# Another order for the first loads of a fused linear-attention and gated-MLP kernel

## The chip, the cores and the metric

The kernel runs on one core of a Trainium2 chip. Five engines work side by side on it, each with its own stream of instructions: PE (matmul), ACT (the scalar engine), DVE (the vector engine), POOL (GpSimd) and SP, which here only issues DMAs. Engines wait for each other through semaphores. The metric is the device time of one execution in microseconds; less is better. Before the change it was 221.64 us (median of three runs, 221.39 to 222.84).

## What is computed

The reference normalises x (2048 tokens of 512 values) and adds two branches to it. Cut to what matters:

```
xn = layernorm(x)                                   # 2048 x 512
q, k, v = split(xn @ wqkv)                          # 32 heads of 16
phi(a)  = [softmax(a @ w_phi), softmax(-a @ w_phi)] # per head, 16 + 16 features
kv, z   = sum_s phi(k)_s v_s^T,  sum_s phi(k)_s
attn    = (phi(q) kv) / (phi(q) z + 1e-6) @ wo
mlp     = ((xn @ w_gate) * (xn @ w_up)) @ w_down    # hidden width 1792
out     = x + attn + mlp
```

## The kernel before

Tokens are cut into 16 tiles of 128 (t = 0 to 15) and, for the MLP, into 4 groups of 512 (g); the hidden width into 14 column tiles of 128 (ft). A contraction over 512 is four matmuls (q = 0 to 3) that add up in one PSUM bank. These kinds of work return in the prediction:

- **Normalisation.** For t = 0 to 3 DVE takes the moments of the raw tile (L415, L416; the mean of t = 1 comes from ACT, L423), subtracts the mean (L430), PE transposes the centred tile by a product with the identity (four matmuls of 128 columns) and ACT copies it out (L277). For t = 4 and up DVE takes moments for four tiles at once (L452, L454), POOL makes the reciprocal root (L458, L460), DVE normalises (L481) and a DMA transpose puts the result into the transposed array.
- **k_pe(t)**: the value projection, four matmuls against `wv`, copied by ACT.
- **wprime(w)**: folds `w_phi` into the key (w = 1) or query (w = 0) weights: 16 matmuls of 128 columns, with a block-diagonal form of `w_phi` that POOL builds first (L395). After it **k_pk(t)** and **q_pk(t)** give the features in four matmuls; ACT makes both signs, DVE a tree of maxima (L519) and a subtraction (L525), ACT the exponential, DVE the sums (L539), a reciprocal (L568) and the product (L571). For keys the last three are k_norm(t).
- **glu(g, ft)**: a gate product and an up product, four matmuls of 512 columns each; ACT copies the gate out of its bank, DVE multiplies it with the up bank (L595) and so frees that bank. The units share three PSUM banks at first (5, 6, 7), later four, so a product waits for the ACT copy or the DVE multiply of an earlier unit.
- **emit_kv(half)**: sums over the key tiles of one half, 8 groups of 8 small matmuls. **q_num(t)** and **final(t)** finish the attention and the output.

All matmuls are issued by one helper, L297, all ACT copies by L277 and all DMAs by L165 (L164 for transposes).

The order of the work is not the order of the source. Each operation is recorded as a step; a planner (`_order`) then gives each engine a fixed order, by list scheduling on assumed costs. For a DMA the recorded argument `at` is the earliest time at which the planner takes the data to have landed. It changes nothing in the DMA itself, only where the planner puts the steps that use the data. Each engine works off its list strictly in order, and waits at the head of it.

All loads are issued by SP. The first ones of the kernel before are: x tiles 0, 1, and 2 with 3 in one transfer; the value weights in two halves of 256 rows; gate and up columns of the first four column tiles; x tiles 4 to 7; the feature weights `w_phi`; then the transposing load of the key weights, and the other gate and up columns. x tiles 8 to 15 are issued only when the DMA transpose of tile 7 has landed (`load_later`), with an assumed landing of 29.8 us.

k_pe(0) to k_pe(3) are recorded matmul by matmul, so that the planner may begin them with the rows that a first half of the value weights holds.

Of the kernel before, what the change touches and what calls it, by code (L numbers as in the profile page):

```python
# [12 lines left out]
PE, ACT, DVE, POOL, SP = "PE", "ACT", "DVE", "POOL", "SP"  # L13
# [168 lines left out]
def bass_parallel_sum__linear_kernel_hedgehog__glu_gated_bilinear__prompt_kernel(  # L182
    nc: bass.Bass,
    A_x: bass.AP,
    A_wqkv: bass.AP,
    A_w_phi: bass.AP,
    A_wo: bass.AP,
    B_x: bass.AP,
    B_w_gate: bass.AP,
    B_w_up: bass.AP,  # L190
    B_w_down: bass.AP,
    out: bass.AP,
):
    with ExitStack() as es:
        _build(nc, es, A_x, A_wqkv, A_w_phi, A_wo, B_w_gate, B_w_up, B_w_down, out)


def _build(nc, es, A_x, A_wqkv, A_w_phi, A_wo, B_w_gate, B_w_up, B_w_down, out):
# [59 lines left out]
    def sbv(name, lo, n):  # L258
        off = layout[name] + lo
        return arena[:, off:off + n]  # L260
# [67 lines left out]
    wv_v = sbv("wv", 0, NQ * 512).rearrange("p (q j) -> p q j", q=NQ)  # L328
    wo_v = sbv("wo", 0, NQ * 512).rearrange("p (q j) -> p q j", q=NQ)
    wg_v = sbv("wg", 0, NQ * FF).rearrange("p (q f) -> p q f", q=NQ)  # L330
    wu_v = sbv("wu", 0, NQ * FF).rearrange("p (q f) -> p q f", q=NQ)
# [4 lines left out]
    def load_x(on, t0, n, at):  # L336
        return sc.dma(on, sbv("x", t0 * 512, n * 512).rearrange("p (t d) -> p t d", t=n),
                      x_flat[t0 * 128:(t0 + n) * 128, :].rearrange("(t p) d -> p t d", p=128), at=at)

    def load_w(on, dst, src, at, issue=500.0):  # L340
        return sc.dma(on, dst, src, at=at, issue=issue)

    def load_wT(w, at):

        return sc.dma(SP, wT_v[:, w, :, :], A_wqkv[:, w * 512:(w + 1) * 512], transpose=True, at=at, issue=4600.0)

    def load_gu(on, f0, n, at):
        return [load_w(on, v[:, :, f0 * 128:(f0 + n) * 128],
                       src[:, f0 * 128:(f0 + n) * 128].rearrange("(q p) f -> p q f", p=128), at)
                for v, src in ((wg_v, B_w_gate), (wu_v, B_w_up))]  # L350

    load_x(SP, 0, 1, 2950.0)
    load_x(SP, 1, 1, 3400.0)
    load_x(SP, 2, 2, 4700.0)
    wv_loads = [load_w(on, wv_v[:, 2 * h:2 * h + 2, :],
                       A_wqkv[h * 256:(h + 1) * 256, 1024:1536].rearrange("(q p) j -> p q j", p=128), at)
                for on, h, at in ((SP, 0, 5700.0), (SP, 1, 6600.0))]
    load_gu(SP, 0, 4, 9300.0)
    load_x(SP, 4, 4, 11400.0)
    sc.dma(SP, wphi_v, bass.AP(tensor=A_w_phi.tensor, offset=A_w_phi.offset, ap=[[16, 128], [2048, NQ], [1, 16]]),  # L360
           at=11600.0)
    load_wT(1, 13600.0)
    load_gu(SP, 4, 5, 17900.0)
    load_gu(SP, 9, 5, 22300.0)


# [568 lines left out]
```

## Time and profile before

| | before |
|---|---|
| time, median of three runs | 221.64 us (221.39 to 222.84) |
| profiled execution: span, first to last instruction | 219.2 us |
| granted TensorE clock, mean | 1.000 |
| HBM read, written | 8.67 MB, 2.10 MB |
| POOL busy | 10.7 us |

The span is what the page gives of the profiled execution's own time; the median of the runs is 2.4 us more, for what lies before the first and after the last instruction. Times in the profile count from the start of the span. Matmuls overlap, so a busy PE row does not tell how tightly they follow each other; that is read from the starts. In lists of instructions the bracket gives how long the engine sat idle before the instruction and what ended that.

### The profile page before, as it was taken

Reading aid. Unit: us, or ns where it says so; the run is one execution under the profiler, and the core shown is the slowest. Engines: PE = TensorE matmul, PEld = TensorE weight load, DVE = VectorE, ACT = ScalarE, POOL = GpSimd, SP = SyncE. Lnnn points to the kernel's source line nnn. Section 1 sums busy time; section 2 is a strip of 40 time slices with the busy share of each in tenths; the row PEclk is TensorE's granted clock in tenths of the full one; section 3 lists DMA queues with packets and bytes.
Section 4 is the critical chain, followed back from the end, with each engine's and each line's share of the span. In section 5 each row is a group of like instructions: output and inputs, shape, how many; then the busy total and the mean of one; then the engine's idle time right before and its main releaser. Section 6 shows DMA issues by size and latency. Waiting matters only on the chain.

```text
span 219.2 us, 3572 instructions
## 1 busy us (share of the span) xinstructions
PE 215.1 (98%) x1281; PEld 105.0 (48%) x1281; DVE 193.0 (88%) x549; ACT 115.5 (53%) x191; POOL 10.7 (5%) x29
## 2 busy tenths in 40 slices
PE   7999999999999999999999999999999999999995
PEld 6444444444445545444445444445444445444543
DVE  4477999999999389999999899999999999998432
ACT  4757987548453599965452885735453333230000
POOL 4431000010002000000000000000000000000000
DMA  5999550025901340000000003155367555656451
GB/s 169 325 227 354 95 178 1 3 56 145 326 0 23 78 96 3 0 0 0 3 0 1 3 0 65 30 99 106 80 129 99 121 119 119 100 122 141 96 76 48
DMA packets 47458, 19.91 MB, mean 91 GB/s; under 512 B 37456, under 2 KB 47440, under 8 KB 47440
## 3 DMA queue, kind: packets, MB, share of 16 engines
q1 hardware_dynamic: 47440, 19.69, 39.6%
q8 instruction: 10, 0.16, 0.3%
q14 instruction: 8, 0.07, 0.1%
HBM read 8.67 MB, written 2.10 MB: 49 GB/s over the span
## 4 chain that ended last, share of the span: by engine, by line
PE 96%; DMA 2%; SPq 1%; issue 0%; DVE 0%
PE ps L297 96%; DMA arena<-in_A_wqkv_dram 2%; SPq L165 1%; DVE arena L700 0%
## 5 line engine op out<-in xcount | busy, mean ns | idle before, releaser
L297 PE MATMUL ps<-arena 128*128 128x512 bf16 (+4 forms) x1281 | 215.1, 331 | 1.8 <-DVE arena L368 1.0
L297 PEld LDWEIGHTS ps<-arena 128*128 128x128 bf16 x1281 | 105.0, 99 | 111.8 <-ACT arena L277 1.3
L277 ACT ACTIVATE arena<-ps 128x512 bf16<-128x512 f32 (+1 forms) x136 | 71.8, 590 | 48.3 <-PE ps L297 40.0
L277 ACT ACTIVATE arena<-arena 128x1024 bf16<-128x1024 bf16 (+1 forms) x40 | 38.5, 977 | 28.4 <-DVE arena L525 28.3
L539 DVE TENSOR_TENSOR arena<-arena 128x512 f32<-128x512 bf16 (+3 forms) x128 | 49.0, 394 | 0.2
L595 DVE TENSOR_TENSOR arena<-ps,arena 128x512 bf16<-128x512 f32 x56 | 38.1, 680 | 2.7 <-PE ps L297 1.6
L519 DVE TENSOR_TENSOR arena<-arena 128x64 bf16<-128x64 bf16 (+3 forms) x128 | 31.4, 273 | 4.0 <-ACT arena L277 3.7
L525 DVE TENSOR_TENSOR arena<-arena 128x1024 bf16<-128x1024 bf16 x32 | 21.5, 676 | 0.1
L700 DVE TENSOR_TENSOR arena<-ps,arena 128x512 bf16<-128x512 f32 (+2 forms) x13 | 8.4, 648 | 7.1 <-PE ps L297 6.9
L452 DVE BATCH_NORM_STATS2 arena<-arena 128x6 f32<-128x512 bf16 x12 | 8.2, 688 | 3.5 <-DMA arena<-in_A_x_dram 3.5
L571 DVE TENSOR_TENSOR arena<-arena 128x1024 bf16<-128x1024 bf16 x16 | 10.9, 680 | 0.0
L277 ACT ACTIVATE arena<-ps,arena 128x512 bf16<-128x512 f32 x12 | 7.8, 682 | 2.8 <-PE ps L297 2.8
L568 DVE RECIPROCAL arena<-arena 128x64 bf16<-128x64 f32 x16 | 8.7, 546 | 0.0
L672 DVE TENSOR_TENSOR arena<-ps,arena 128x512 bf16<-128x512 f32 x12 | 8.1, 675 | 0.1
L664 DVE RECIPROCAL arena<-ps 128x32 f32<-128x32 f32 x16 | 5.6, 348 | 2.4 <-PE ps L297 2.4
L651 DVE TENSOR_TENSOR arena<-arena 128x512 bf16<-128x512 bf16 x16 | 6.6, 415 | 0.0
L648 DVE RECIPROCAL arena<-arena 128x32 f32<-128x32 f32 x16 | 5.4, 335 | 0.0
L481 DVE TENSOR_SCALAR arena<-arena 128x512 bf16<-128x512 bf16 x12 | 4.3, 401 | 0.5 <-POOL arena L460 0.5
L415 DVE BATCH_NORM_STATS2 arena<-arena 128x6 f32<-128x512 bf16 x4 | 2.8, 690 | 2.0 <-DMA arena<-in_A_x_dram 2.0
L458 POOL TENSOR_SCALAR arena<-arena 128x4 f32<-128x4 f32 x3 | 0.8, 259 | 50.7 <-DVE arena L454 50.7
L460 POOL TENSOR_TENSOR arena<-arena 128x4 f32<-128x4 f32 x3 | 3.2, 1051 | 0.3
L697 DVE SCALAR_TENSOR_TENSOR arena<-ps,arena 128x512 bf16<-128x512 f32 x4 | 3.0, 748 | 0.0
(29 smaller groups left out, 24.4 us busy)
## 6 DMA issues: line engine op xcount, KB each, us to landing
out_dram<-arena SPq DMA_DIRECT2D x15, 128.0 KB, 1.8
arena<-in_B_w_down_dram SPq DMA_DIRECT2D x1, 1792.0 KB, 7.5
arena<-in_B_w_gate_dram SPq DMA_DIRECT2D x2, 640.0 KB, 6.8
arena<-in_B_w_up_dram SPq DMA_DIRECT2D x2, 640.0 KB, 8.0
arena<-in_A_x_dram SPq DMA_DIRECT2D x1, 1024.0 KB, 6.2
arena<-arena SPq DMA_TRANSPOSE x44, 2.9
arena<-in_A_wqkv_dram SPq DMA_DIRECT2D x2, 256.0 KB, 3.6
arena<-in_B_w_gate_dram SPq DMA_DIRECT2D x1, 512.0 KB, 5.5
```

Source lines behind the costliest of these rows:

```text
L277: return e.activation(out=out_ap, in_=in_ap, func=func, scale=scale, **kw)
L297: ins = e.matmul(o, lhsT=l, rhs=r, start=a, stop=z)
L452: dve(lambda e, t=t: e.bn_stats(stats_v[:, t, 0:6], x_tile(t)), [x_tile(t)], [stats_v[:, t, 0:6]], 512)
L519: dve(lambda e, dst=dst, src=src, k=k: e.tensor_tensor(out=dst, in0=src[:, :, 0:k], in1=src[:, :, k:2 * k], op=ALU.max), [src], [dst], 16 ...
L525: dve(lambda e: e.tensor_tensor(out=p4, in0=p4, in1=src[:, :, None, :].to_broadcast([128, 16, 16, 4]), op=ALU.subtract), [pst, src], [pst] ...
L539: dve(lambda e, dst=dst, src=src, k=k: e.tensor_tensor(out=dst, in0=src[:, :, 0:k], in1=src[:, :, k:2 * k], op=ALU.add), [src[:, :, 0:2 * ...
L568: dve(lambda e: e.reciprocal(out=rs, in_=sm), [sm], [rs], 64, rate=6.0)
L571: dve(lambda e: e.tensor_tensor(out=e4, in0=e4, in1=r4[:, :, None, :].to_broadcast([128, 16, 16, 4]), op=ALU.mult), [ek_v[:, t, :], rs], [ ...
L595: dve(lambda e: e.tensor_tensor(out=dst, in0=bank(bu), in1=gr, op=ALU.mult), [bank(bu), gr], [dst], 512, prio=-1.0)
L651: dve(lambda e: e.tensor_tensor(out=e1, in0=e1, in1=rs[:, :, None, :].to_broadcast([128, 8, 16, 4]), op=ALU.mult), [e1, rs], [e1], 512, ra ...
L672: dve(lambda e: e.tensor_tensor(out=o4, in0=n4, in1=w4, op=ALU.mult), [nd[:, :, 0:64], w], [o], 512)
L700: dve(lambda e: e.tensor_tensor(out=og, in0=ob, in1=xs, op=ALU.add), [ob, xs], [og], c1 - c0, prio=-2.0)
```

## The change

Only the first loads differ. x tiles 2 and 3 come in two transfers instead of one; the value weights come whole instead of in two halves, and stand between them; the feature weights go ahead of x tiles 4 to 7. The number of DMAs (14 up to the last gate and up columns) and the bytes are the same. The assumed landings change too: the gate columns from 9.3 to 9.0 us, the up columns from 9.3 to 10.6 us, the feature weights from 11.6 to 10.9, x 4 to 7 from 11.4 to 12.2, the key weights from 13.6 to 14.0 us. Since the planner works with these, the order on PE, ACT and DVE changes in many places behind the start. The number of instructions on each of them stays the same.

```diff
-    def load_gu(on, f0, n, at):
+    def load_gu(on, f0, n, at, at_up=None):
         return [load_w(on, v[:, :, f0 * 128:(f0 + n) * 128],
-                       src[:, f0 * 128:(f0 + n) * 128].rearrange("(q p) f -> p q f", p=128), at)
-                for v, src in ((wg_v, B_w_gate), (wu_v, B_w_up))]
+                       src[:, f0 * 128:(f0 + n) * 128].rearrange("(q p) f -> p q f", p=128), a)
+                for v, src, a in ((wg_v, B_w_gate, at), (wu_v, B_w_up, at if at_up is None else at_up))]
 
     load_x(SP, 0, 1, 2950.0)
     load_x(SP, 1, 1, 3400.0)
-    load_x(SP, 2, 2, 4700.0)
-    wv_loads = [load_w(on, wv_v[:, 2 * h:2 * h + 2, :],
-                       A_wqkv[h * 256:(h + 1) * 256, 1024:1536].rearrange("(q p) j -> p q j", p=128), at)
-                for on, h, at in ((SP, 0, 5700.0), (SP, 1, 6600.0))]
-    load_gu(SP, 0, 4, 9300.0)
-    load_x(SP, 4, 4, 11400.0)
+    load_x(SP, 2, 1, 3850.0)
+    load_w(SP, wv_v, A_wqkv[:, 1024:1536].rearrange("(q p) j -> p q j", p=128), 5500.0)
+    load_x(SP, 3, 1, 5950.0)
+    load_gu(SP, 0, 4, 9000.0, 10600.0)
     sc.dma(SP, wphi_v, bass.AP(tensor=A_w_phi.tensor, offset=A_w_phi.offset, ap=[[16, 128], [2048, NQ], [1, 16]]),
-           at=11600.0)
-    load_wT(1, 13600.0)
+           at=10900.0)
+    load_x(SP, 4, 4, 12200.0)
+    load_wT(1, 14000.0)
     load_gu(SP, 4, 5, 17900.0)
     load_gu(SP, 9, 5, 22300.0)
```

## The prediction

> **What bounds the kernel now.** I read the page's busy table first, then the chain that ended last in order of time, then the start as a timeline, then the engines by stages.
>
> ```profile
> PE 215.1 (98%) x1281; PEld 105.0 (48%) x1281; DVE 193.0 (88%) x549; ACT 115.5 (53%) x191; POOL 10.7 (5%) x29
> ```
>
> The chain, as start, length and what:
>
> ```profile
> 2.69 4.04 DMA arena<-in_A_wqkv_dram
> 6.72 0.05 issue
> 6.77 210.16 PE ps L297 x1235
> ```
>
> The end is set by the second half of the value weights, which lands at 6.73 (2.69 + 4.04), and from then on by PE alone. Between 20.7 and 44.8 us PE starts 113 matmuls of 512 columns, 24.1 / 112 = 0.216 us apart; a product of four takes 0.863. Read by starts, PE waits after 4 us only at four places: 0.47 before the first and 0.35 before the second half of the value weights, 0.14 at 13.4, 0.10 at 14.4. So about 1.1 us is the most that the change can win; every new wait on PE is a loss.
>
> The start (start, length, instruction, idle before and what ended it):
>
> ```profile
> 4.35 0.90 PE L297 MATMUL ps<-arena 128*128 128x128 bf16 x12 [0.31 <-DVE arena L430]
> 5.56 1.03 PE L297 MATMUL ps<-arena 128*128 128x512 bf16 x7 [0.31 <-DMA arena<-in_A_wqkv_dram]
> 5.71 0.69 DVE L415 BATCH_NORM_STATS2 arena<-arena 128x6 f32<-128x512 bf16 x1
> 6.65 0.35 DVE L430 TENSOR_SCALAR arena<-arena 128x512 bf16<-128x512 bf16 x1
> 6.77 7.45 PE L297 MATMUL ps<-arena 128*128 128x512 bf16 x36 [0.18 <-DMA arena<-in_A_wqkv_dram]
> ```
>
> Loads, with KB and us from issue to landing:
>
> ```profile
> arena<-in_A_x_dram SPq DMA_DIRECT2D x1, 1024.0 KB, 6.2
> arena<-in_A_wqkv_dram SPq DMA_DIRECT2D x2, 256.0 KB, 3.6
> arena<-in_B_w_gate_dram SPq DMA_DIRECT2D x1, 512.0 KB, 5.5
> arena<-in_B_w_up_dram SPq DMA_DIRECT2D x1, 512.0 KB, 6.9
> arena<-in_A_x_dram SPq DMA_DIRECT2D x1, 512.0 KB, 7.8
> arena<-in_A_x_dram SPq DMA_DIRECT2D x1, 256.0 KB, 2.8
> ```
>
> With the issues at 1.71 (x 2, 3), 2.18 and 2.65 (value weights), 3.20 (gate), 3.71 (up), 4.26 (x 4 to 7), 4.81 (feature weights) they land at 4.5, 5.4, 6.7, 8.7, 10.6, 12.06 and 12.3: in their order, as one stream.
>
> DVE, which is nearly as full as PE, where the order changes; and PE, PEld, DVE, ACT, POOL busy by stages:
>
> ```profile
> 20.31 1.24 DVE L519 TENSOR_TENSOR arena<-arena 128x512 bf16<-128x512 bf16 x4 [0.76 <-ACT arena L277]
> 32.78 0.69 DVE L452 BATCH_NORM_STATS2 arena<-arena 128x6 f32<-128x512 bf16 x1
> 35.81 0.68 DVE L595 TENSOR_TENSOR arena<-ps,arena 128x512 bf16<-128x512 f32 x1
> ```
> ```profile
> 45.00:71.00 26.00, 26.00 (x136) 12.03 (x134) 25.91 (x68) 13.80 (x22) 1.27 (x2) 1.00 0.39 114
> 71.00:77.00 6.00, 6.00 (x76) 3.53 (x73) 2.08 (x5) 3.29 (x12) 0.00 (x0) 1.00 0.40 80
> ```
>
> From 21 to 71 us DVE has no room to make up a delay; from 71 to 77 it has 3.9 us.
>
> **The loads, to 10 us.** x 2 takes half of what x 2, 3 took behind x 1 (x 1 is there at 3.39, 4.5 - 3.4 = 1.1, half 0.55): 3.95. DVE reaches it at 4.50 as before; nothing is won. The whole value weights take the two halves' 2.25 (6.73 - 4.5) and land at 6.2; with the gate-to-up step instead (10.6 - 8.7 = 1.9 for the same 512 KB) 5.85. x 3 closes the same 1024 KB as before: 6.7; bounds 6.2 and 7.0.
>
> PE's order here: two matmuls of k_pe(0), the transpose of x 2 (4 x 0.056 = 0.22), five matmuls, the transpose of x 3, nine matmuls. Before, the first three matmuls ran on the first half ahead of 6.77, so 13 and one transpose were left: 6.77 + 13 x 0.216 + 0.22 = 9.80. After: 6.2 + 7 x 0.216 + 0.22 = 7.93, then the transpose waits for x 3: moments to centred tile took 5.71 to 7.00, so 6.75 + 1.29 + 0.06 = 8.1. Then 0.22 and 9 x 0.216: 10.27. **+0.47**; with the early bounds 9.8 (0.0), with x 3 at 7.0 10.55 (+0.75). I take the middle, since the stream was steady.
>
> **Two small waits go.** Both gate products now come before the up product, needed at 12.0 and not 10.67; the up columns land at 10.6, so no wait either way. The third gate product no longer follows at once on a bank that DVE must free (-0.14), and wprime, which waited for POOL's block-diagonal form (12.40 + 1.84 = 14.24), comes at 15.4, with w_phi landing earlier (-0.10). x 4 to 7 land 0.3 later (what w_phi takes, 12.3 - 12.06); DVE has idled 3.5 us there. Issues on SP: the same ten, each hidden behind the stream. PE after the start: 0.47 - 0.24 = **+0.22**.
>
> **The order from 17 us.** The gate product of (0, 4) moves ahead of k_pk(0 to 3), the up product of (0, 5) behind k_pk(4 to 7). So k_pk(0) comes 0.86 + 0.22 = 1.08 later and DVE's tree starts at 21.4 instead of 20.31: idle that DVE cannot use. k_pe(4) comes 0.64 earlier, 24.12; its transposed tile landed at 24.1, behind the weights in the stream (0 to 0.2; I take 0).
>
> On DVE the moments of x 8 (L452) move ahead of seven instructions, the multiply of (0, 5), the end of k_norm(1) and a part of k_norm(2): 0.60 + 0.13 + 0.61 + 0.46 + 0.28 + 0.59 + 0.21, together 2.9 us by their starts. Their load is issued at 25.71, when the transpose of tile 7 has landed, and takes 6.2: 31.9. Before, DVE came at 32.78 and did not wait. From 20.31 to 32.78 it had 12.4 us of work; without those 2.9 it arrives at 21.4 + 9.5 = 30.9 and **waits 0.95, and all of DVE stands behind it**. At 32.5 it then has 2.9 us in hand that were done at 33.38: 32.5 - 33.38 + 2.9 = 2.0 us late.
>
> Who waits for that: PE's gate product of (0, 7) needs the bank of (0, 5), whose multiply ends after 0.60 + 0.13 + 0.10 + 0.60 + 0.68 at 34.0, plus 0.06; PE is there at 33.40 + 0.22 = 33.62: **+0.45**. The up product of (0, 8) needs the multiply of (0, 7), which ends 3.7 after that, 37.7; PE is there at 34.07 + 4 x 0.863 = 37.52: **+0.24**. Later multiplies have more room (0.56 to 1.5 before). The first emit_kv waits for k_norm(7), whose product ended at 70.13 for a start at 70.52. After, one more product stands before it on PE (70.52 + 0.86 + 0.91 = 72.29) and a multiply for a normalisation on DVE (70.13 + 2.0 + 0.27 = 72.40): **+0.1**. Then DVE's idle stretch ends the delay.
>
> Behind 77 us products are exchanged again, the second emit_kv comes two products later on PE (slack 0.25 before, 1.98 after), and each late q_num a third of a final later; I take 0, between 0 and +0.5. The last operations are the same.
>
> Sum: 0.22 + 0.45 + 0.24 + 0.1 = **+1.0 us**: span 220.2, and with the 2.4 us around it the median of 221.64 becomes **222.6**. From 33 us on the start hardly matters: the time follows the landing of x 8 to 15, us for us.
>
> A rule to weigh: PE idles from 5.09 to 6.2 in one piece. In the profile the longest idle after the first matmuls is some 0.5 us, and behind it 128-column matmuls keep 0.056 us (0.107 in the first 2.7 us; the granted clock reads 1.00 throughout, so only the starts show it). [...]
>
> **Cases.** One per cent (219.4 to 223.9) is about what a measurement of this kernel tells from no change.
> 1. The forecast, +0.5 to +1.6: 0.58.
> 2. DVE is not blocked, or the stream carries x 3 at 6.2: start -0.24, DVE's margins hold; for it speaks that the plan's own landings (5.5, 5.95) lie there, against it the 2.25 us of the halves and that the planner takes x 8 at 29.8 and gets it at 31.9. -0.4 to +0.4, about 221.6: 0.22.
> 3. Slower by over 1%, at one place: the transposes of tiles 4 to 7, whose issue starts 1.3 later (DVE's normalisation at 18.9, not 17.57, since the moments before it now stand behind a later multiply), land later and with them x 8 to 15. They took 5.84 us to issue in four; 19.35 + 5.84 + 1.84 to landing is 27.0, against 25.7. Then x 8 to 15 land at 33.2, DVE is 3.3 late and PE at the first emit_kv 3.3 + 0.27 - 1.26 = 2.3: 223.9. It decides from 33.1 on. Against it: the second issue alone took 1.97, in a full queue, the others 1.21 to 1.27, and a later start finds it emptier. 0.14.
> 4. The clock falls in the idle piece: half of the first 2.7 us again, +1.4, which takes the place of the later waits: 223.2. 0.04.
> 5. Faster by over 1%: only 1.1 us of waits is there to win. 0.02.
>
> The range reaches over the second case and half of the third: 221.2 to 224.0. Faster 0.02, same 0.82, slower 0.16.
>
> **What shows it.** Right: PE's value projection starts at 5.9 to 6.2 and its glu at 10.0 to 10.4; a DVE wait for the x DMA near 31 us; waits of PE on L595 near 34 and 37. Wrong, if x 3 is there by 6.2, if that DVE wait is missing, if x 8 lands after 33, or if PE shows waits behind 77.

## The result, and the profile after

| | before | after |
|---|---|---|
| time, median of ten executions each | 221.44 us (220.63 to 222.84) | 222.79 us (222.56 to 226.4) |
| ratio, 95% interval | | 1.0094 (1.0073 to 1.0116) |
| profiled execution: span | 219.2 us | 220.9 us |
| profiled execution: start of the last matmul | 216.70 us | 217.90 us |
| from there to the end of the span | 2.5 us | 3.0 us |

The changed kernel takes 222.79 us where 222.6 was forecast. The medians are 1.35 us apart, 0.6%; the ratio of 0.9% lies nearer to that of the means, which the slowest executions raise. Ratios and intervals here leave out executions more than 1.5% above the fastest of the same kernel, which are the one of 226.4 and in experiment 4 the one of 226.2. Six of the ten executions lie at 222.56 to 222.89 us, the profiled one (222.7) among them, and four at 224.2 to 226.4; experiments 4, 7, 9 and 10 bear on what makes those four.

The page of the kernel after, its busy times and the chain that ended last:

```profile
PE 214.3 (97%) x1257; PEld 105.3 (48%) x1281; DVE 192.5 (87%) x549; ACT 115.5 (52%) x191; POOL 10.7 (5%) x29
...
PE 64%; DVE 24%; DMA 7%; issue 2%; SPq 1%; ACT 1%; DVEq 0%
```

PE's busy time says little (24 of its matmuls left no record). The chain does: before, one piece of PE work ran from 6.77 us to the end; now the chain leaves PE for DVE and for DMAs. In order of time (start, length, what), after:

```profile
2.66 3.94 DMA arena<-in_A_x_dram
...
6.63 0.71 DVE arena L414
...
8.13 8.39 PE ps L297 x53
...
23.24 3.62 DMA arena<-arena
26.87 5.23 DMA arena<-in_A_x_dram
32.13 0.70 DVE arena L451
...
33.66 0.59 DVE arena L594
...
37.38 0.61 DVE arena L594
38.04 1.04 PE ps L297 x4
```

Each place at which it leaves PE ahead of 40 us is a step of the prediction: the first DMA is x 3, for whose transpose PE waits until 8.13; then, from 23.24, come the DMA transposes of the later tiles, behind them the load of x 8 to 15, and behind that the moments (L451, before L452) and two multiplies (L594, before L595), for each of which PE waits. From 142.63 to 191.38 the chain runs over DVE once more, and over one store; the prediction did not name that, but PE's starts show no wait there, so it costs nothing. (Lines of the kernel after are one less than before's from the loads on.)

The start, as a timeline of PE and DVE (start, length, instruction; in brackets the idle time before and what ended it):

```profile
4.29 1.26 PE L297 MATMUL ps<-arena 128*128 128x128 bf16 x12 [0.18 <-DVE arena L429]
...
6.39 2.98 PE L297 MATMUL ps<-arena 128*128 128x512 bf16 x18 [0.84 <-DMA arena<-in_A_wqkv_dram]
6.63 0.69 DVE L414 BATCH_NORM_STATS2 arena<-arena 128x6 f32<-128x512 bf16 x1 [0.85 <-DMA arena<-in_A_x_dram]
...
7.58 0.35 DVE L429 TENSOR_SCALAR arena<-arena 128x512 bf16<-128x512 bf16 x1
```

The value weights start the products at 6.39 instead of 5.56 (half) and 6.77 (the other half). x 3 lands at 6.60, DVE centres it by 7.93, and its transpose follows at 8.12. The first glu product, seen in PE's starts, comes at 10.29 instead of 9.81.

The loads after, with KB and us from issue to landing:

```profile
arena<-in_A_x_dram SPq DMA_DIRECT2D x1, 1024.0 KB, 5.2
...
arena<-in_A_wqkv_dram SPq DMA_DIRECT2D x1, 512.0 KB, 4.1
arena<-in_B_w_gate_dram SPq DMA_DIRECT2D x1, 512.0 KB, 5.5
```

DVE between 30 and 38 us, after:

```profile
30.82 0.22 DVE L518 TENSOR_TENSOR arena<-arena 128x128 bf16<-128x128 bf16 x1
32.13 0.70 DVE L451 BATCH_NORM_STATS2 arena<-arena 128x6 f32<-128x512 bf16 x1 [1.09 <-DMA arena<-in_A_x_dram]
...
33.57 0.68 DVE L594 TENSOR_TENSOR arena<-ps,arena 128x512 bf16<-128x512 f32 x1
...
37.30 0.69 DVE L594 TENSOR_TENSOR arena<-ps,arena 128x512 bf16<-128x512 f32 x1
```

DVE has nothing else to do for 1.09 us, because the moments of x 8 stand at the head of its list. The multiplies of (0, 5) and (0, 7) behind it are the ones that PE waits for: in PE's starts 0.484 us at 33.6 and 0.272 us at 37.55. The first of the two stands in PE's timeline as well, as the idle time before 34.30 (0.32 us, less than 0.484 because the recorded end of a matmul, 0.38 us after its start, lies behind the next start, 0.216 after it):

```profile
34.30 8.01 PE L297 MATMUL ps<-arena 128*128 128x512 bf16 x34 [0.32 <-DVE arena L594]
```

After that PE never waits again but for 0.06 us at 128.9, which was there before too (0.057). DVE makes up the rest where the prediction looked for it; PE, PEld, DVE, ACT, POOL busy by stages, after:

```profile
45.00:71.00 26.00, 25.89 (x120) 11.78 (x121) 26.00 (x69) 14.10 (x22) 0.40 (x2) 1.00 0.38 112
71.00:77.00 6.00, 5.90 (x55) 3.20 (x55) 4.04 (x9) 2.31 (x7) 1.18 (x2) 1.00 0.28 58
```

Its idle time from 71 to 77 us falls from 3.9 to 2.0 us. The prediction did not read the end. DVE's last additions, before (L700) and after (L699):

```profile
215.95 0.56 DVE L700 TENSOR_TENSOR arena<-ps,arena 128x384 bf16<-128x384 f32 x1 [1.10 <-PE ps L297]
216.95 0.29 DVE L700 TENSOR_TENSOR arena<-ps,arena 128x128 bf16<-128x128 f32 x1 [0.45 <-PE ps L297]
```
```profile
216.50 0.69 DVE L699 TENSOR_TENSOR arena<-ps,arena 128x512 bf16<-128x512 f32 x1 [3.83 <-PE ps L297]
217.93 0.75 DVE L699 TENSOR_TENSOR arena<-ps,arena 128x384 bf16<-128x384 f32 x2 [0.74 <-PE ps L297]
```

The last tile is finished in two parts, of 384 and of 128 columns. Before, the last matmuls of the larger part came ahead of the smaller part's, so DVE added 384 columns at 215.95 while PE still worked, and only 0.29 us followed the last matmul. After, the planner has put the third piece of the larger part next to last. DVE adds both parts behind the end of PE, 0.75 us in one go, and the last store is issued at 218.90 instead of 217.27: 1.63 us later, 1.20 of it from PE.

### The profile page after: what moved, and what is told of

Same layout as the page of the kernel before. It is cut to its first block, busy times and chain, and to the rows that moved or that the text cites. A ratio compares the mean times of both kernels' runs of the same rounds, so it can differ in the third digit from the quotient of the medians.

```text
span 220.9 us, 3541 instructions
## 1 busy us (share of the span) xinstructions
PE 214.3 (97%) x1257; PEld 105.3 (48%) x1281; DVE 192.5 (87%) x549; ACT 115.5 (52%) x191; POOL 10.7 (5%) x29
## 4 chain that ended last, share of the span: by engine, by line
PE 64%; DVE 24%; DMA 7%; issue 2%; SPq 1%; ACT 1%; DVEq 0%
PE ps L297 64%; DVE arena L538 6%; DMA arena<-in_A_x_dram 4%; DVE arena L518 3%; DVE arena L524 3%; DVE arena L671 2%; DVE arena L699 2%; DMA arena<-arena 2%; DVE arena L594 2%; DVE arena L650 1%; DVE arena L668 1%; DVE arena L663 1%; DVE arena L647 1%; DMA out_dram<-arena 1%; SPq L165 1%
## 5 line engine op out<-in xcount | busy, mean ns | idle before, releaser
L277 ACT ACTIVATE arena<-arena 128x1024 bf16<-128x1024 bf16 (+1 forms) x40 | 38.8, 978 | 27.4 <-DVE arena L524 27.3
L594 DVE TENSOR_TENSOR arena<-ps,arena 128x512 bf16<-128x512 f32 x56 | 37.8, 678 | 5.0 <-PE ps L297 4.9
L699 DVE TENSOR_TENSOR arena<-ps,arena 128x512 bf16<-128x512 f32 (+2 forms) x13 | 8.3, 644 | 7.7 <-PE ps L297 6.8
L451 DVE BATCH_NORM_STATS2 arena<-arena 128x6 f32<-128x512 bf16 x12 | 8.1, 688 | 3.6 <-DMA arena<-in_A_x_dram 3.6
L570 DVE TENSOR_TENSOR arena<-arena 128x1024 bf16<-128x1024 bf16 x16 | 10.9, 681 | 0.0
```

Of the source, the lines that this page charges most:

```text
L277: return e.activation(out=out_ap, in_=in_ap, func=func, scale=scale, **kw)
L451: dve(lambda e, t=t: e.bn_stats(stats_v[:, t, 0:6], x_tile(t)), [x_tile(t)], [stats_v[:, t, 0:6]], 512)
L570: dve(lambda e: e.tensor_tensor(out=e4, in0=e4, in1=r4[:, :, None, :].to_broadcast([128, 16, 16, 4]), op=ALU.mult), [ek_v[:, t, :], rs], [ ...
L594: dve(lambda e: e.tensor_tensor(out=dst, in0=bank(bu), in1=gr, op=ALU.mult), [bank(bu), gr], [dst], 512, prio=-1.0)
L699: dve(lambda e: e.tensor_tensor(out=og, in0=ob, in1=xs, op=ALU.add), [ob, xs], [og], c1 - c0, prio=-2.0)
```

## The experiments

Ten kernels were run, in three sets, each beside runs of the kernel before on the same chip. Where an order is said to be written out, the planner's lists are replaced by fixed lists for every engine. "From the first value product to the last matmul" is read from PE's starts; it leaves out when the value weights land, which differs from one execution to the next.

### 1. The new loads, in the old order

```diff
 loads: as in the kernel after
-order on every engine: the planner's
+order on every engine: that of the kernel before, written out
```

> The new loads with the engine orders of the kernel before (its PE, ACT, DVE and POOL lists written out). Theory: the loads alone cost the wait for the third x tile, +0.47 us at the start, and save the 0.10 us at the folded key weights; the moments of x 8 stand where they stood, DVE does not wait for that load, and the last operations are as before. Span 219.5, time 0.1 to 0.2% above before. Rival (the value weights in one piece are what costs): span 220.5 to 220.9, like the changed kernel.

Measured: 221.3 us against 221.23, ratio 1.0002 (0.9991 to 1.0013); span 219.4. The last matmul starts at 216.90, 0.21 later than before. From the first value product to it are 210.53 us, against 211.51 in the kernel after. The loads alone cost nothing that the time shows; what they cost PE is what the prediction gave them (0.22).

### 2. The old loads, in the new order

```diff
 loads: as in the kernel before
-order on every engine: the planner's
+order on every engine: that of the kernel after, written out
```

> The old loads with the engine orders of the changed kernel. Theory: the start ends within 0.1 us of before (14 matmuls behind the second half instead of 13, +0.22, less the two small waits, 0.24); then the same losses as in the changed kernel: 0.2 at the transposed tile 7, 0.75 by the wait of DVE for x 8 to 15, 0.5 at the last stores. Span 220.6, 0.6 to 0.7% above before. Rival (the loads cost it): span 219.2 to 219.4.

Measured: 222.79 us, ratio 1.0076 (1.0062 to 1.009). In its profiled execution (223.59 us, its slowest) the second half of the value weights landed at 7.84 instead of 6.72, so its span of 221.9 is not to be compared; the waits are. The chain in order of time (start, length, what):

```profile
24.09 3.63 DMA arena<-arena
...
27.74 5.31 DMA arena<-in_A_x_dram
...
33.07 0.69 DVE arena L452
```

The same path as after, the transposes, x 8 to 15, the moments, and behind it the same waits of PE: 0.196 at 27.4, 0.560 at 34.5, 0.274 at 38.5. So the cost is the order's, whichever loads stand before it.

### 3. The end put right

```diff
 PE, the last steps (1100, 1101: parts of the 384 columns; 1104 to 1106: the 128 columns)
-1100 1096 1104 1105 1101 1106
+1100 1096 1101 1104 1105 1106
```

> The changed kernel with one exchange on PE: the third part of the last 384 output columns goes back ahead of the first two parts of the last 128, as it stood before. Theory: the last add no longer stands behind the 384-column add, nor its store behind the issue of that store: span 220.45, 0.2% below the changed kernel. Rival (the end is set by the last store's landing anyway): span 220.9.

Measured: 222.23 us, ratio 1.0064 (1.0039 to 1.0088), span 220.2. DVE's last additions, in this kernel:

```profile
216.35 1.21 DVE L699 TENSOR_TENSOR arena<-ps,arena 128x512 bf16<-128x512 f32 x2 [3.83 <-PE ps L297]
218.00 0.29 DVE L699 TENSOR_TENSOR arena<-ps,arena 128x128 bf16<-128x128 f32 x1 [0.45 <-PE ps L297]
```

Only the 128 columns are left behind PE, and from the last matmul (217.75) to the end are 2.50 us instead of 3.04. The exchange of three steps is worth about 0.5 us, and the waits of 0.41 and 0.27 at 33.5 and 37.4 are still there. Two of the six executions, 223.54 and 223.64, lie above the others.

### 4. The moments moved on DVE

```diff
 DVE, from 31 us on
-moments of x 8, sum and tree of two key tiles, moments of x 9, multiply (0, 5), ... multiply (0, 6), ...
+sum and tree of two key tiles, multiply (0, 5), ... multiply (0, 6), moments of x 8, moments of x 9, ...
```

> The changed kernel with two instructions moved on DVE: the moments of x 8 and x 9 stand behind the multiply of (0, 6) instead of ahead of the multiply of (0, 5). Theory: DVE no longer waits 1.1 us near 31 us, the PE waits of 0.48 near 33.6 and 0.27 near 37.6 go, and nothing comes in their place: span 220.15, 0.35% below the changed kernel. Rival (DVE is late because its exponent chain starts 1.08 later, whatever stands in front): PE waits of about the same sum come back later, span 220.7 to 220.9.

Measured: 224.3 us, ratio 1.0111 (1.0076 to 1.0145): missed. The two waits on PE went, but the moved moments, 1.2 us together, now stood ahead of the multiply of (0, 7), which ended at 41.51, and PE waited 0.692 for that at 40.66. So little was to be won (0.07). That is read from one execution with a late start, the slowest of the six, and its span is not to be compared; the two lowest executions, 222.36 and 222.54, are 0.1 to 0.2 below the kernel after and agree with it. The other four, at 224 to 226.2, are something else. PE at the start of the profiled one (226.2 us):

```profile
2.72 2.95 PE L297 MATMUL ps<-arena 128*128 128x128 bf16 x23
7.28 3.15 PE L297 MATMUL ps<-arena 128*128 128x512 bf16 x10 [1.62 <-DMA arena<-in_A_wqkv_dram]
10.65 4.65 PE L297 MATMUL ps<-arena 128*128 128x128 bf16 x18 [0.22 <-issue]
```

From 7.28 to 10.4 it records 10 matmuls where the kernel after has 18 in as long a stretch. Matmuls of 512 columns follow at 0.427 us, of 128 at 0.107, until 13.2 us; then 0.216 and 0.056 again. The granted clock reads 1.00 in all stages of the profile; the last section comes back to that. This is near to the prediction's fourth case, and the next sets look at it.

### 5. The up columns not assumed later

```diff
-    load_gu(SP, 0, 4, 9000.0, 10600.0)
+    load_gu(SP, 0, 4, 9000.0)
```

> The changed kernel with one number taken out: the planner takes the up columns to land at 9.0 us like the gate columns, not at 10.6. The DMAs are issued exactly as in the changed kernel; the planner's orders come out nearly as before. Theory (the later landing told to the planner sets the new order, and the new order costs): 221.3 to 221.5, like the kernel with only the loads changed, 0.0 to 0.15% above before, no DVE wait near 31 us and the last operations as before. Rival (it is the landings of x 4 to 7 and of the other loads that move the order for the worse): 222.4 to 222.8.

Measured: 221.49 us, ratio 1.0032 (1.001 to 1.0055), span 219.6. Eight of twelve executions lie at 221.27 to 221.62, four at 222.76 to 223.35; the four raise the ratio. The DMAs are those of the kernel after; only the planner is told that the up columns land with the gate columns. Its chain in order of time:

```profile
2.17 4.25 DMA arena<-in_A_wqkv_dram
6.42 0.14 issue
6.55 210.76 PE ps L297 x1242
217.31 0.02 issue
217.34 0.29 DVE arena L699
```

One piece of PE work again, 210.53 us from the first value product to the last matmul, as in experiment 1, and the short end. So of all the assumed landings that the change alters, the one of the up columns set the costly order, at both places. It is the truer one: told 10.6, the planner got them at 10.35 us in the kernel after, while here, told 9.0, it got them at 9.98.

### 6. The planner told when x 8 to 15 land

```diff
-            load_later(lambda: load_x(SP, 8, 8, 29800.0))
+            load_later(lambda: load_x(SP, 8, 8, 32100.0))
```

> The changed kernel with one other number: the planner takes x 8 to 15 to land at 32.1 us, where they do, not at 29.8. Its orders stay those of the changed kernel except behind 31 us on DVE, where the moments of x 8 go behind nine more instructions. Theory: the DVE wait of 1.1 us and the PE waits of 0.48 and 0.27 go, the 0.18 at tile 7 and the 0.5 at the last stores stay: span 220.15, 0.35% below the changed kernel. Rival (DVE is late by its later start, not by the wait): PE waits of the same sum, span 220.7 to 220.9.

Measured: 222.27 us, ratio 1.0059 (1.0033 to 1.0085), span 220.4. DVE between 32 and 38 us in this kernel:

```profile
32.54 0.68 DVE L594 TENSOR_TENSOR arena<-ps,arena 128x512 bf16<-128x512 f32 x1
...
34.93 0.68 DVE L594 TENSOR_TENSOR arena<-ps,arena 128x512 bf16<-128x512 f32 x1
...
36.20 0.68 DVE L594 TENSOR_TENSOR arena<-ps,arena 128x512 bf16<-128x512 f32 x1
...
37.34 0.68 DVE L451 BATCH_NORM_STATS2 arena<-arena 128x6 f32<-128x512 bf16 x1
```

The moments come behind three multiplies and wait for nothing; of PE's waits between 20 and 70 us 0.09 is left. From the first value product to the last matmul are 210.64 us, 0.87 less than after. The span is 0.25 over what was expected; the value products began at 6.70 in this execution, not 6.39. The end is the long one (3.0 us). Five of the twelve executions lie at 223.28 to 224.04, the others at 221.78 to 222.45. The new number moves more than the moments: in the order that experiment 9 writes out from it, 92 places of DVE's list, 20 of ACT's and 12 of PE's differ from the kernel after. Experiment 8 leaves the lists alone.

### 7. The idle piece before the value weights filled

```diff
-            mms([(bank(7, 0, 128), zero, zero, True, True)] * 4, cold=True).deps.append(sc.by_eng[PE][-2])
+            mms([(bank(7, 0, 128), zero, zero, True, True)] * 14, cold=True).deps.append(sc.by_eng[PE][-2])
```

The order is that of the kernel after, written out; the ten further products multiply zeros.

> The changed kernel, its orders written out, with 14 instead of 4 products of zeros behind the transpose of x 1, so that PE is busy for most of the 1.0 us in which it waits for the value weights; nothing else waits for them. Theory (single executions of the changed kernel at 224 us and more are those in which the clock of PE is still at half behind that idle piece, as the trace with the moved moments shows until 13.2 us): no execution above 223.7, the others at 222.4 to 222.8. Rival (they come from value weights that land a microsecond later): as many executions at 224 and more as without the products, 3 or 4 in 10.

Measured: 223.0 us (222.82 to 223.22), ratio 1.008 (1.0064 to 1.0096), span 221.3. No execution lies above the others. All six are somewhat above the 222.6 of the kernel after; in the profiled one the value products began 0.32 later (6.71), and x 8 to 15 landed 0.37 later:

```profile
32.50 0.70 DVE L451 BATCH_NORM_STATS2 arena<-arena 128x6 f32<-128x512 bf16 x1 [1.15 <-DMA arena<-in_A_x_dram]
```

From the first value product to the last matmul are 211.54 us, as after (211.51). Why the value weights come later here is open.

### 8. The moments of x 8 and 9 without their load

```diff
-            dve(lambda e, t=t: e.bn_stats(stats_v[:, t, 0:6], x_tile(t)), [x_tile(t)], [stats_v[:, t, 0:6]], 512)
+            xt = x_tile(t - 4 if t in (8, 9) else t)
+            dve(lambda e, t=t, xt=xt: e.bn_stats(stats_v[:, t, 0:6], xt), [xt], [stats_v[:, t, 0:6]], 512)
```

The order is that of the kernel after, written out. The moments of tiles 8 and 9 are taken from tiles 4 and 5, so the right normalisation of two tiles is left out and the instructions stay the same.

> The changed kernel, its orders written out, with the moments of x 8 and x 9 taken from tiles 4 and 5, which have long landed: the same instructions at the same places, without the wait for the load (the result for tiles 8 and 9 is normalised with the moments of other tiles). Theory: DVE goes on at 31.0 instead of 32.1, the multiply of (0, 5) ends at 33.2 and of (0, 7) at 36.9, before PE needs them: both PE waits, 0.76 together, go; span 220.15, 0.35% below the changed kernel. Rival: other waits take their place, span 220.7 to 220.9.

Measured: 222.3 us, ratio 1.0055 (1.0031 to 1.0078), span 220.6. DVE in this kernel:

```profile
31.43 0.22 DVE L519 TENSOR_TENSOR arena<-arena 128x128 bf16<-128x128 bf16 x1
31.56 0.69 DVE L452 BATCH_NORM_STATS2 arena<-arena 128x6 f32<-128x512 bf16 x1
...
33.00 0.67 DVE L595 TENSOR_TENSOR arena<-ps,arena 128x512 bf16<-128x512 f32 x1
```

The same list of instructions, with the wait gone from its middle. PE has no wait left after 7 us but the 0.06 at 128.6, and 210.55 us lie between the first value product and the last matmul: 0.96 less than after. Of that, 0.18 is the wait at the transposed tile 7, which is absent here because PE, having begun at 7.00, came there later; the rest, 0.78, is the DVE wait's. The late beginning is also why the span is 0.45 over the expected one. One of the seven executions (224.12) lies above the others.

### 9. Both repairs together

```diff
-            load_later(lambda: load_x(SP, 8, 8, 29800.0))
+            load_later(lambda: load_x(SP, 8, 8, 32100.0))
 PE, the last steps
-1100 1096 1104 1105 1101 1106
+1100 1096 1101 1104 1105 1106
```

The order is that of experiment 6, written out, with the three steps exchanged.

> The changed kernel with the two repairs together: the planner is told that x 8 to 15 land at 32.1 us, and the last matmul of the 384-column part stands again ahead of the 128-column part's. If the waits for x 8 to 15 and the order at the end are the whole of what the changed kernel lost, little of the loss is left: from the first product of the value weights to the last matmul 210.6 us, as with the first repair alone, and 2.5 us from there to the end of the span, as in the kernel before, instead of 3.0. With the value weights landed between 6.25 and 6.6 us that is a span of 219.5 to 219.8, a median of 221.3 to 221.7 us and a ratio of 1.001 to 1.003. If instead the new order costs something in a place that I have not seen, the time stays at 222 us or more.

Measured: 221.72 us (221.34 to 223.77) against 221.4, ratio 1.0032 (1.0002 to 1.0061). Seven executions lie at 221.34 to 221.8, in the expected range, five at 223.01 to 223.77. The profiled one is of the five (223.08), and so shows what those are. PE at its start:

```profile
4.33 1.46 PE L297 MATMUL ps<-arena 128*128 128x128 bf16 x12 [0.23 <-DVE arena L429]
6.46 3.15 PE L297 MATMUL ps<-arena 128*128 128x512 bf16 x10 [0.67 <-DMA arena<-in_A_wqkv_dram]
9.83 5.46 PE L297 MATMUL ps<-arena 128*128 128x128 bf16 x27 [0.22 <-issue]
```

As in experiment 4: 10 matmuls in 3.15 us, spacings of 0.427 and 0.107, here until 10.04 us. From the first value product to the last matmul are 212.39 us, 1.75 more than in experiment 6, of which it differs only at the end. That is the distance between the two groups of executions.

### 10. Both repairs, and the idle piece filled

```diff
 as 9, and
-            mms([(bank(7, 0, 128), zero, zero, True, True)] * 4, cold=True).deps.append(sc.by_eng[PE][-2])
+            mms([(bank(7, 0, 128), zero, zero, True, True)] * 14, cold=True).deps.append(sc.by_eng[PE][-2])
```

> The same with 14 instead of 4 zero products after the transposes of x 1, which cover most of PE's idle time before the value weights. If executions that lie 1.3 us and more above the others come from PE's clock, which an idle piece of 1 to 1.5 us before the value weights leaves low for longer, none is seen here: all executions within 0.6 us of each other, at 221.3 to 221.9, while the kernel without the ten products shows some at 222.7 and above. If they come from something else, some are seen here too.

Measured: 221.56 us (221.19 to 223.14), ratio 1.0001 (0.9975 to 1.0027). Eleven of twelve executions lie at 221.19 to 221.85, one at 223.14. With experiment 7 that is 1 execution in 18 in the upper group where the piece is filled, against 5 of 12 here without the ten products; so "none" was too much, though they are fewer. Counted over everything that was run, executions at least 1.3 us above the lowest of their set are 25 of 76 with the new loads and four zero products (none of the 11 of experiment 1), 1 of 18 with fourteen, none of the 6 of experiment 2 with the old loads, and 5 of 76 in the kernel before, so they are not the changed kernel's alone. Nothing is faster than the kernel before: what the repairs take away is what the change had brought.

## Why the prediction was right

By its own steps, in the profiled execution after:

| step | predicted | measured |
|---|---|---|
| first glu product, behind x 3 | 10.27, +0.47 | 10.29, +0.47 |
| two small waits go | -0.24 | -0.24 |
| transposed tile 7 | 0 | +0.183 |
| bank of (0, 5) | +0.45 | +0.484 |
| up product of (0, 8) | +0.24 | +0.272 |
| first emit_kv | +0.1 | 0 |
| behind 77 us | 0 (0 to 0.5) | 0.00 |
| last matmul | +1.0 | +1.20 |
| the last operations | 0 | +0.5 |
| span | 220.2 | 220.9 |
| around the span | 2.4 | 1.8 |

- **The loads.** x 2 was put at 3.95, the value weights at 6.2, x 3 at 6.7; they landed at 3.80, 6.25 and 6.60. Experiment 1 has the sum of this part by itself, +0.21 against +0.22. The list of PE's waits before leaves one out, 0.50 us before 4.35 for the centred x 1; it is still there after (0.44 before 4.29), so the sum is not touched.
- **The wait for x 8 to 15** is the core of it, and held: DVE came to the moments at 31.0 (30.9 predicted) and waited 1.09 us (0.95), and experiment 8 shows it as the cause by reading another tile in the same order; experiment 6, with a later place, agrees. The landing itself was right by two misses that cancel. The load was issued 1.16 later than the sum had it, 26.87 instead of 25.71, since the transposes of tiles 4 to 7 came later, as the third case said they would; and it flew 5.2 us, not 6.2. That the two cancel is luck. It landed at 32.10, and the third case needed 33.1.
- **Tile 7** is the other side of that delay: its transpose landed at 26.86, not 25.69. The prediction weighed only tile 4 against PE (0 to 0.2, and it took 0). The term was mis-sized by 0.18.
- **The second case** fell with x 3 at 6.60 and the DVE wait. **The fourth** put a clock that falls in the idle piece, PE's wait for the value weights, at +1.4. The sum took nothing for it; that was the author's estimate, since the longest idle in the trace before, behind its first matmuls, was 0.5 us. In the profiled execution after, the rate held across 1.01 us, with 0.216 us per 512 columns behind it. The profiles of experiments 4 and 9 show a rate that had not yet risen, 0.427 us per 512 columns behind the piece; in 9 it cost 1.75. The four at 224.2 to 226.4 are 1.5 to 3.7 above the profiled one; no profile was taken of them, so that they are such executions is argued from experiments 4, 7, 9 and 10, not shown. One number bears on it: the mean granted clock of the one at 225.07 is 0.992, which over its span of 223.3 us makes 1.8 us lost, an estimate, and the three other executions with 0.992 (224.04 in experiment 6, 223.77 in 9, 223.85 of the kernel before) are each the slowest of their set. Because of the four the median stands at 222.79, not at the 222.6 of the other six.
- **The step that failed** is "The last operations are the same": the instructions are the same, their order on PE is not, and that cost 0.5 us, as experiment 3 shows by putting it back. It did not show in the forecast time because of an error the other way, so that the time came out so near is partly luck. The 2.4 us around the span came from setting the profiled span against the median of other executions; after, 1.8 us lie around it, and all ten experiments' profiles have 1.7 or 1.8. So the profiled execution before was one of about 221.0, an estimate, and the sum started 0.6 too high. For the same reason the two profiled spans are 1.7 apart, while the six executions at 222.6 lie only 1.2 above the median before.

The change's cost is thus one decision of a planner with two consequences: with the up columns assumed later (experiment 5), a product moves, DVE's moments and PE's last steps change places, and 0.94 us of waits and 0.5 us at the end follow. That the assumption was the truer one did not help, because the landing that mattered, that of x 8 to 15, was still assumed 2.3 us too early. That holds for the waits; the end stayed long in experiment 6, where this landing was put right, and why the planner reverses PE's last steps is open.

## What to carry to other kernels

Where a fixed order is worked out from assumed landings, correcting one of them can cost more than it tells: look first for the assumed landing that is furthest from the trace, and ask what stands at the head of an in-order engine's list when it is missed. Read the end of the order as carefully as the start, since there nothing is left behind which a late step could hide. And set a span only against the time of the same execution: the 0.6 us lost there are more than half of the effect forecast here.

## What the runs showed of the hardware

**The matmul rate stayed at half for 10 and 13 us after the start in two executions.** PE's first matmuls of 128 columns follow at 0.107 us, and at 0.056 from a moment that differs from one profiled execution to the next (4.35 us before, 5.20 after). Where that moment lay ahead of the idle piece before the value weights, the rate stayed up across it (1.48 us of idle in experiment 5, and 0.216 us per 512 columns behind it). In the two profiled executions in which it had not come when PE went idle, for 1.87 us in experiment 4 and 0.93 in experiment 9 (1.62 and 0.67 from the recorded ends), it came only at 13.2 and 10.04 us, 5.9 and 3.6 us after PE went on. That the idle pieces held it back is a reading of these two executions; by what rule it comes was not shown. The profile's stages read a granted clock of 1.00 in all of it, because time for which a trace holds no clock record counts as full there: the trace before holds none, and its mean reads 1.000 with the matmuls at 0.107 us in it. After, the record begins where the spacing halves, at 5.20 us. Why experiment 1, with the same idle piece (0.91 us in PE's timeline, 0.84 after), had no such execution in eleven is open.

**The same load lands at other times.** With the same loads in the same order the value products began between 6.38 us (experiment 1) and 7.28 (experiment 4) in the profiled executions, and what follows moved with them: in one and the same order, x 8 to 15 were issued at 26.87 us where the products began at 6.39 (after), and at 27.32 where they began at 7.00 (experiment 8). x 8 to 15 took 6.2 us before, 5.2 after and 5.2 to 5.5 in experiments 2, 3, 6, 7 and 8. Differences of a few tenths between two profiles are to be read from there on, not from the start of the span.
